# Two issuing queues at the start of a gated decode kernel, and the order of the first turnings

## The chip, the core and the metric

The kernel runs on one core of one Trainium2 chip. The metric is the device time of one execution in microseconds (us), the median of several runs. The engines are PE (matrix products; PEld is its weight load), DVE (vector), ACT (scalar functions), POOL and SP. SP and ACT can issue DMAs, each on a queue of its own; sixteen DMA engines move the data.

## The reference

One token goes through two branches, attention over a sliding window of a cache and a dense layer with gelu, mixed by a gate. Cut to what matters:

```python
# x: 1 x 576; 32 query heads, 16 key/value heads of 128; window W = 4096
q = (x @ wq)                                   # 576 x 4096 -> 32 heads
k = k_cache[:, :, Sk - W:, :]                  # 16 heads x 4096 x 128
v = v_cache[:, :, Sk - W:, :]
scores = einsum("bhqd,bhkd->bhqk", q, k) * Dh ** -0.5
a = (softmax(scores) @ v).reshape(1, 1, 4096) @ wo
b = gelu(x @ w1 + b1) @ w2 + b2                # 576 -> 4608 -> 576
g = sigmoid((x * gate_w).sum())
out = g * a + (1 - g) * b
```

All arrays are bf16. The window of keys and of values is 16.8 MB each, and with the weights 53.6 MB are read from HBM.

## The kernel before

**Tiles of keys and values.** The 16 key/value heads are taken four at a time: four tiles of keys (k0 to k3) and four of values (v0 to v3), 4 MB each. Every tile is one DMA (`load_kv`, L104): 128 partitions, each with one row of 32 KB. They take turns in a pool of three buffers (`kv_pool`, L80), which also holds the two halves of w2 at the end. So a tile can only be issued when an earlier one has been used up. The weights w_q, w1 and w_o share one buffer (`w_pool`, L81) in turn.

**Order of the DMAs.** All are issued by SP, in this order, except b2, which ACT issues (L140): the first part of w_q (512 KB), k0, x, the larger part of w_q (4096 KB), k1, b1 in two pieces, a row of x, gate_w, k2, then v0, k3, w1, v1, v2, v3, w_o and w2. The larger part of w_q comes behind k0 and x by `load_flat` (L120), which calls `first_keys` (L142) between its two pieces.

**x and the query.** x is loaded as 64 short rows of nine numbers, `x9` (L144). One product with `dup` (L384) and four DVE steps (L392) spread it over the partitions as `x2`, the stationary operand of the query products and later of w1. The query takes 36 products (L401), in nine steps over four column groups; the first four need only the first part of w_q, the other 32 the larger part. Then DVE and ACT copy the query from PSUM (L413, L419), 16 small products turn it (L425), and four DVE copies (L437) lay it into `qz`, the stationary operand of the scores.

**Turnings and scores.** A tile of keys is cut into four chunks (UT = 4). `transposes(h)` (L249) turns chunk h on DVE into a buffer `kT`, of which there are four (L83). `scores(h)` (L271) multiplies the chunk by `qz` in eight products. Chunks 0 to 3 are of k0, 4 to 7 of k1, and so on.

**What sets the order.** The schedule is by hand (`manual_schedule`, L90): every engine runs its instructions in the order of the program text. On DVE this is: constants, `transposes(0)`, the spread of x, `transposes(1)` to `transposes(3)`, the copies of the query, and then, chunk by chunk, the turning of the tile after the one whose scores are running, with the steps of the softmax (L290 to L322) between. `v0` is issued after `transposes(3)`, because it takes the buffer of k0; k3 after `transposes(7)`, v1 after `transposes(11)`, v2 after the products with v0 (`values(0)`), v3 after `transposes(15)`.

**The end.** After the values (L341) and their sums, `part` collects in PSUM (L672) half of w_o, the first half of w2 and the rest of w_o; DVE and ACT copy it (L680, L681). The second half of w2 comes in four pieces; its rows are multiplied one by one (L652), the copies of `part` are added by eight products after the thirteenth row (L692), and the result is copied (L701) and stored (L702).

Of the kernel before, what the change touches and what calls it, by code (L numbers as in the profile page):

```python
# [9 lines left out]
BF16 = mybir.dt.bfloat16  # L10
# [6 lines left out]
def kernel(  # L17
# [15 lines left out]
    nc = tc.nc  # L33

    P = 128
# [10 lines left out]
    UT = 4  # L46
# [9 lines left out]
    NQ = 4  # L56
# [6 lines left out]
    NM = 9  # L63


    QC = Hq * Dh // 8
# [14 lines left out]
    w_pool = ctx.enter_context(tc.tile_pool(name="w_pool", bufs=1))  # L81
# [11 lines left out]
    wq_flat = A_wq.rearrange("a b -> (a b)").rearrange("(p n) -> p n", p=P)  # L93
# [7 lines left out]
    def load_kv(cache, m, name):  # L101
        t = kv_pool.tile([P, NCK, Dh], BF16, name=name, tag="kv")

        nc.sync.dma_start(  # L104
            out=t[:],
            in_=cache[0, HT * m : HT * (m + 1), Sk - W : Sk, :].rearrange(
                "e (p c) d -> p e (c d)", c=NCK
            ),
        )
        return t  # L110

    def load_k(m):
        return load_kv(A_k_cache, m, "k_t")

    def load_v(m):
        return load_kv(A_v_cache, m, "v_t")

    WMAX = F * D // P

    def load_flat(src, name, cuts=(), between=None):  # L120
        n = src.shape[1]
        t = w_pool.tile([P, WMAX], BF16, name=name, tag="w")
        edges = (0, *cuts, n)
        for i, (a, b) in enumerate(zip(edges, edges[1:])):
            if i == 1 and between is not None:
                between()
            nc.sync.dma_start(out=t[:, a:b], in_=src[:, a:b])
        return t

    k_tiles, v_tiles = {}, {}  # L130

    x9 = const.tile([P // 2, NM], BF16, name="x9")
# [6 lines left out]

    nc.scalar.dma_start(out=b2_r[:], in_=B_b2.rearrange("(o n) -> o n", o=1))  # L140

    def first_keys():  # L142
        k_tiles[0] = load_k(0)
        nc.sync.dma_start(out=x9[:], in_=A_x.rearrange("a b (i m) -> (a b i) m", m=NM))  # L144

    wq_t = load_flat(wq_flat, "wq_t", (NQ * QC,), first_keys)

    k_tiles[1] = load_k(1)  # L150
    b1_r = const.tile([P, 2, FB], BF16, name="b1_r")
    nc.gpsimd.memset(b1_r[:], 0.0)
    for o in range(2):
        nc.sync.dma_start(
            out=b1_r[o : o + 32 * (NQ - 1) + 1 : 32],
            in_=B_b1.rearrange("(o t k n) -> o t k n", o=2, t=NQ, k=2)[o],
# [18 lines left out]
        out=row_f[:], in_=ident_f[:, 0 : 32 * (NQ - 1) + 1 : 32], axis=AX.X, op=ALU.add  # L175
# [5 lines left out]
        out=dup[:].rearrange("k (i e) -> k i e", e=2),  # L181
        in_=ident[0 : P // 2, 0 : P // 2].rearrange("k (i e) -> k i e", e=1).to_broadcast(
            [P // 2, P // 2, 2]
        ),
    )
    par = const.tile([P, 2], FP32, name="par")
    for o in range(2):
        nc.vector.tensor_reduce(
            out=par[:, o : o + 1],
            in_=ident_f[:].rearrange("p (i o) -> p o i", o=2)[:, o, :],  # L190
# [7 lines left out]
    for o in range(NOG):  # L198
        nc.vector.tensor_copy(
            out=spread_o[:, o, :].rearrange("k (t r q) -> k t r q", t=NT // NOG, q=QD),  # L200
            in_=ident[:, (P // NOG) * o : (P // NOG) * (o + 1)].rearrange("k (t x u) -> k t x u", x=32, u=1)[
                :, :, 0:R, :
            ].to_broadcast([P, NT // NOG, R, QD]),
# [5 lines left out]
        out=m_r[:, 0:R], in_=ident_f[:].rearrange("p (s r) -> p r s", r=R), axis=AX.X, op=ALU.add  # L209
# [8 lines left out]
        out=off[:], in_=ident_f[:].rearrange("p (x g q) -> p g x q", g=HT, q=2), axis=AX.XY,  # L218
# [3 lines left out]
        out=off[:], in0=off[:], scalar1=1.0e30, scalar2=-1.0e30, op0=ALU.mult, op1=ALU.add  # L222
# [4 lines left out]
        out=m_c[:], in_=ident_f[:].rearrange("p (t c r) -> p c t r", c=BC, r=R), axis=AX.XY,  # L227
# [4 lines left out]
        out=m_q[:], in_=ident_f[:].rearrange("p (h q) -> p q h", q=QD), axis=AX.X, op=ALU.add  # L232
# [7 lines left out]
        out=sel[:].rearrange("p l (o h) -> p l o h", o=2),  # L240
        in_=ident[:].rearrange("p (h l x) -> p l x h", h=2, l=2)[:, :, 0:2, :],
# [4 lines left out]
    def transposes(h):  # L246
        kT[h] = kT_pool.tile([P, NCH * ND], FP32, name="kT", tag="kT")
        lo = (h % UT) * NCH * Dh
        nc.vector.transpose(  # L249
            out=kT[h][:],  # L250
            in_=k_tiles[h // UT][:].rearrange("p c d -> p (c d)")[:, lo : lo + NCH * Dh].bitcast(
                FP32
            ),
        )
# [123 lines left out]

    transposes(0)

    x_ps = ps_m.tile([P, NM], FP32, name="x_ps", tag="m")
    nc.tensor.matmul(x_ps[:], lhsT=dup[:], rhs=x9[:], start=True, stop=True)  # L384
    ev, od = par[:, 0:1], par[:, 1:2]
# [5 lines left out]
    ):  # L391
        nc.vector.tensor_scalar(out=dst, in0=src, scalar1=s, scalar2=None, op0=ALU.mult)  # L392

    for h in range(1, UT):
        transposes(h)
    v_tiles[0] = load_v(0)

    q_ps = ps_a.tile([P, 2, 512], FP32, name="q_ps", tag="a")
    for b in range(NM * NQ):
        m, t = b // NQ, b % NQ  # L400
# [10 lines left out]
    for i in range(NI):  # L411
        copy = nc.scalar.copy if i % 2 else nc.vector.tensor_copy
        copy(  # L413
            out=q_r[:, i].rearrange("p (b o) a u -> p b o a u", b=2)[:, :, :, 0, :],
            in_=q_ps[:, 0, i * Dh : (i + 1) * Dh].rearrange("p (b u o) -> p b o u", b=2, o=2),
        )
    for i in range(NI):
        copy = nc.scalar.copy if i % 2 else nc.vector.tensor_copy
        copy(  # L419
            out=q_r[:, i, :, 1:NA, :],  # L420
            in_=q_r[:, i, :, 0:1, :].to_broadcast([P, NBP, NA - 1, PI]),
# [12 lines left out]
    for a in range(NA):  # L434
# [3 lines left out]
            out=qz[rows, lo : lo + NR * QW].rearrange("p (b t w) -> p b t w", b=NBP, w=QW)[  # L438
                :, :, :, 0:R
            ].rearrange("p b t (l i) -> p b t l i", l=2),  # L440
            in_=qT[rows].rearrange("p i b (l t) -> p b t l i", l=2),
# [115 lines left out]

    for h in range(UT):
        scores(h)
# [66 lines left out]
    for o in range(NOG):  # L629
# [3 lines left out]
        out=ow_m[:],  # L633
# [5 lines left out]
    with nc.allow_low_precision("one of the eight summands is not zero"):  # L639
        nc.vector.tensor_reduce(  # L640
            out=ow[:].rearrange("p j o -> p o j"),
            in_=ow_m[:].rearrange("p o q j -> p o j q"), axis=AX.X, op=ALU.add,
# [90 lines left out]
```

## Time and profile before

| | |
|---|---|
| median of 3 runs | 133.25 us (133.07 to 133.31) |
| the profiled execution | 133.64 us |
| its span, first to last instruction | 131.8 us |
| DVE busy | 73.9 us, 56% of the span |
| PE busy | 71.9 us, 55% |
| ACT busy | 9.6 us, 7% |
| read from HBM | 53.62 MB, 407 GB/s over the span |
| chain that ended last, by engine | DVE 35%, DMA 30%, PE 27% |

A group of the profile has a line (L401 is line 401 of the kernel), an engine, an operation and its operands. A timeline line gives start, duration, engine, line and operands, and in brackets how long the engine had stood idle before and what ended that. A line of waits gives who waited for whom: the sum in us, how many times, the longest. The chain of work that ended last is followed back from the last instruction to whatever released each step; it says what the end waited for, not what was busiest. The row of the DMA engines gives their busy share in tenths in 40 equal slices of the span.

### The profile page before, as it was taken

What the parts mean: (1) busy time and instruction counts of PE and PEld (TensorE: products, weight loads), DVE (VectorE), ACT (ScalarE), POOL (GpSimd) and SP (SyncE); (2) the same over time, 40 slices, a digit from 0 to 9 for tenths busy, and PEclk for the clock granted to TensorE, in tenths of its full rate; (3) what the DMA queues carried; (4) which work ended last, traced back from release to release, by engine and by line L of the source; (5) the groups of instructions that cost most, each with busy time, mean ns of one, the idle gap of its engine ahead of it and who ended that gap; (6) DMA issues with size and microseconds to landing.
All of it is one profiled execution on the core that took longest, in us unless ns stands there. A gap on an engine that the chain in (4) does not pass through costs nothing.

```text
span 131.8 us, 1417 instructions
## 1 busy us (share of the span) xinstructions
PE 71.9 (55%) x590; PEld 30.4 (23%) x590; DVE 73.9 (56%) x114; ACT 9.6 (7%) x19; POOL 3.9 (3%) x10
## 2 busy tenths in 40 slices
PE   0000010565999668805972882838936547646871
PEld 0000000222344224302431220213613122213441
DVE  2900599323199999995049907164758852670011
ACT  3200000012000002100300000030030000000011
POOL 8300000000000000000000000000000000000000
PEclk9999999999999999996897555555698555995599
DMA  4999998998999899999999999999999999999950
GB/s 103 514 408 408 458 418 388 478 458 369 450 468 433 378 468 448 408 410 512 403 428 403 453 408 438 468 413 408 458 448 398 463 403 475 385 416 420 419 224 0
DMA packets 2557, 53.70 MB, mean 408 GB/s; under 512 B 364, under 2 KB 632, under 8 KB 888
## 3 DMA queue, kind: packets, MB, share of 16 engines
q1 hardware_dynamic: 2550, 53.62, 95.2%
q8 instruction: 4, 0.07, 0.2%
q14 instruction: 1, 0.01, 0.0%
q10 hardware_dynamic: 2, 0.00, 0.0%
HBM read 53.62 MB, written 0.00 MB: 407 GB/s over the span
## 4 chain that ended last, share of the span: by engine, by line
DVE 35%; DMA 30%; PE 27%; issue 3%; SPq 1%; ACT 1%; DVEq 0%
DVE kT L249 20%; DMA wq_t<-in_A_wq_dram 17%; PE s_ps L271 15%; DMA w_t<-in_B_w_dram 13%; PE acc L341 4%; PE q_ps L401 3%; DVE ms L290 3%; PE h_ps L454 2%; DVE mx L295 2%; DVE ez L322 2%; DVE a_s L363 2%; DVE hT L479 1%; PE mb L312 1%; DVE qz L437 1%; PE mT L301 1%
## 5 line engine op out<-in xcount | busy, mean ns | idle before, releaser
L271 PE MATMUL s_ps<-kT,qz 128*128 128x512 bf16 x128 | 39.7, 473 | 10.7 <-DVE kT L249 9.4
L249 DVE STREAM_TRANSPOSE kT<-k_t 128x2048 f32<-128x2048 f32 x16 | 36.2, 2289 | 11.5 <-DMA k_t<-in_A_k_cache_dram 7.8
L271 PEld LDWEIGHTS <-qz 128*128 128x128 bf16 x128 | 14.2, 113 | 32.5 <-issue 22.5
L341 PE MATMUL acc<-v_t,ez 128*32 128x512 bf16 x128 | 11.2, 487 | 0.0
L401 PE MATMUL q_ps<-wq_t,x 128*32 128x512 bf16 x36 | 4.2, 626 | 9.0 <-DMA wq_t<-in_A_wq_dram 6.6
L316 ACT ACTIVATE pr<-ms,nb 128x1024 bf16<-128x1024 f32 x4 | 4.6, 1149 | 60.8 <-DVE nb L313 60.8
L384 PE MATMUL x_ps<-x,dup 64*128 64x9 bf16 x1 | 0.2, 163 | 14.8 <-DMA x<-in_A_x_dram 14.8
L371 PE MATMUL o_ps<-a_s,m_r 128*32 128x128 f32 x8 | 1.9, 319 | 8.2 <-DVE a_s L363 8.2
L290 DVE TENSOR_TENSOR ms<-s_ps,off 128x1024 f32<-128x1024 f32 x4 | 4.8, 1210 | 2.6 <-PE s_ps L271 2.5
L401 PEld LDWEIGHTS <-x 128*32 128x32 bf16 x36 | 1.4, 134 | 20.9 <-issue 20.9
L322 DVE STREAM_TRANSPOSE ez<-pr 128x1024 bf16<-128x1024 bf16 x4 | 4.9, 1220 | 1.4 <-ACT pr L316 1.4
L301 PE MATMUL mT<-ident_f,mx 128*1 128x128 f32 x4 | 1.3, 332 | 7.5 <-DVE mx L295 7.5
L341 PEld LDWEIGHTS <-ez 128*32 128x32 bf16 x128 | 4.2, 114 | 4.2 <-issue 2.5
L295 DVE TENSOR_REDUCE mx<-ms 128x1 f32<-128x1024 f32 x4 | 4.9, 1220 | 0.1
L313 DVE TENSOR_SCALAR nb<-mb 128x1 f32<-128x1 f32 x4 | 0.6, 145 | 7.7 <-PE mb L312 7.7
L680 DVE COPY part<-part 128x288 f32<-128x288 f32 x1 | 0.5, 458 | 7.6 <-PE part L672 7.6
L363 DVE SCALAR_TENSOR_TENSOR a_s<-acc,m_c,a_s 128x128 f32<-128x128 f32 x12 | 4.2, 351 | 0.4
L302 DVE TENSOR_REDUCE m<-mT 1x8 f32<-1x128 f32 x4 | 1.1, 268 | 5.2 <-PE mT L301 5.2
L672 PE MATMUL part<-wo_t,ow 128*1 128x288 bf16 x64 | 4.0, 395 | 0.0
L166 DVE CAST ident_f<-ident 128x128 f32<-128x128 bf16 x1 | 2.2, 2174 | 2.4 <-POOL ident masks.py:199 2.4
L359 DVE TENSOR_SCALAR a_s<-acc,m_c 128x128 f32<-128x128 f32 x4 | 1.3, 330 | 3.7 <-PE acc L341 3.7
L672 PE MATMUL part<-w_t,gt 128*1 128x288 bf16 x36 | 2.6, 440 | 1.5 <-DMA w_t<-in_B_w_dram 1.5
(85 smaller groups left out, 47.2 us busy)
## 6 DMA issues: line engine op xcount, KB each, us to landing
k_t<-in_A_k_cache_dram SPq DMA_DIRECT2D x4, 4096.0 KB, 24.8
v_t<-in_A_v_cache_dram SPq DMA_DIRECT2D x4, 4096.0 KB, 30.2
w_t<-in_B_w_dram SPq DMA_DIRECT2D x1, 5184.0 KB, 31.1
wo_t<-in_A_wo_dram SPq DMA_DIRECT2D x1, 4608.0 KB
wq_t<-in_A_wq_dram SPq DMA_DIRECT2D x1, 4096.0 KB, 22.1
w_t<-in_B_w_dram SPq DMA_DIRECT2D x1, 2592.0 KB, 18.4
w_t<-in_B_w_dram SPq DMA_DIRECT2D x1, 1872.0 KB, 15.5
w_t<-in_B_w_dram SPq DMA_DIRECT2D x1, 576.0 KB, 16.9
```

What stands on the lines that cost most here:

```text
L249: nc.vector.transpose(out=kT[h][:], in_=k_tiles[h // UT][:].rearrange("p c d -> p (c d)")[:, lo : lo + NCH * Dh].bitcast(FP32),)
L271: nc.tensor.matmul(s_tiles[t][:, k].rearrange("p c i e -> p c (i e)"), lhsT=qz[:, r * QW + lo : r * QW + lo + P], rhs=kT_v[:, k * NCB : (k ...
L290: nc.vector.tensor_tensor(out=ms[:], in0=s_v, in1=off[:].rearrange("p (o e) -> p o e", o=1).to_broadcast([P, NCH * 8, HT]), op=ALU.add,)
L295: nc.vector.tensor_reduce(out=mx[:], in_=ms[:].rearrange("p x e -> p (x e)"), axis=AX.X, op=ALU.max)
L301: nc.tensor.transpose(out=mT[:], in_=mx[:], identity=ident_f[:])
L316: nc.scalar.activation(out=pr[:].rearrange("p c j -> p (c j)"), in_=ms[:].rearrange("p x e -> p (x e)"), func=ACT.Exp, bias=nb[:, 0:1], sc ...
L322: nc.vector.transpose(out=ez[:, t].rearrange("p x c r -> p c x r"), in_=pr[:].rearrange("p c j -> p (c j)"),)
L341: nc.tensor.matmul(acc[t][32 * ct : 32 * ct + BC * R, :, :], lhsT=ez[:, t, x, c : c + BC, :].rearrange("p c r -> p (c r)"), rhs=v_tiles[t] ...
L363: nc.vector.scalar_tensor_tensor(out=a_s[:], in0=acc[t][:, c, :], scalar=m_c[:, c : c + 1], in1=a_s[:], op0=ALU.mult, op1=ALU.add,)
L401: nc.tensor.matmul(q_ps[32 * t : 32 * (t + 1), 0, 0:QC], lhsT=x2[:, m, :], rhs=wq_t[:, b * QC : (b + 1) * QC], start=(m == 0), stop=(m == ...
L454: nc.tensor.matmul(h_box[0][32 * t : 32 * (t + 1), k, 0:FB], lhsT=x2[:, m, :], rhs=w[:, off : off + FB], start=(m == 0), stop=(m == NM - 1),)
L672: nc.tensor.matmul(part[32 * t : 32 * t + 1, k, 0:DB], lhsT=col, rhs=w[:, i * D + k * DB : i * D + (k + 1) * DB], start=(n == 0 and t > 0) ...
```

## The change

ACT issues x and the larger part of w_q, on its own queue; SP issues the first part of w_q, k0 and k1 without them in between. In the program text the spread of x now stands ahead of all turnings, then come `transposes(0)` and `transposes(1)`, then the query, and `transposes(2)`, `transposes(3)` and the issue of v0 stand behind the query, right ahead of the first scores. Nothing is added or left out.

```diff
-    def first_keys():
-        k_tiles[0] = load_k(0)
-        nc.sync.dma_start(out=x9[:], in_=A_x.rearrange("a b (i m) -> (a b i) m", m=NM))
-    wq_t = load_flat(wq_flat, "wq_t", (NQ * QC,), first_keys)
+    wq_t = w_pool.tile([P, WMAX], BF16, name="wq_t", tag="w")
+    nc.sync.dma_start(out=wq_t[:, 0 : NQ * QC], in_=wq_flat[:, 0 : NQ * QC])
+    k_tiles[0] = load_k(0)
+    nc.scalar.dma_start(out=x9[:], in_=A_x.rearrange("a b (i m) -> (a b i) m", m=NM))
+    nc.scalar.dma_start(
+        out=wq_t[:, NQ * QC : wq_flat.shape[1]], in_=wq_flat[:, NQ * QC :]
+    )
     k_tiles[1] = load_k(1)
...
-    transposes(0)
-
     x_ps = ps_m.tile([P, NM], FP32, name="x_ps", tag="m")
     nc.tensor.matmul(x_ps[:], lhsT=dup[:], rhs=x9[:], start=True, stop=True)
...
-    for h in range(1, UT):
+    for h in range(2):
         transposes(h)
-    v_tiles[0] = load_v(0)
...
+    for h in range(2, UT):
+        transposes(h)
+    v_tiles[0] = load_v(0)
 
     for h in range(UT):
         scores(h)
```

## The prediction

> **What bounds the kernel now.** I read the DMA line of the page first, then the chain of work that ended last in order of time, then the waits of the last stretch.
>
> ```profile
> DMA  4999998998999899999999999999999999999950
> q1 hardware_dynamic: 2550, 53.62, 95.2%
> ```
>
> The 16 DMA engines are busy from the first slice to the last but two. The trace also keeps one record per DMA packet: one row of a 4 MB load is 32 KB and takes 1.21 us on its engine, the next row begins where the last ended, and I find no idle time from 2.7 us to 126 us. Whatever the kernel does, 53.6 MB need this long; nothing ends before the last piece of w2, which is used at 128.54.
>
> ```profile
> 2.50 22.13 DMA wq_t<-in_A_wq_dram
> ...
> 24.67 3.63 PE q_ps L401 x25
> ...
> 32.03 3.61 PE s_ps L271 x8
> ...
> 35.66 8.94 DVE kT L249 x4
> ...
> 107.80 3.44 PE acc L341 x27
> ...
> 111.64 16.86 DMA w_t<-in_B_w_dram
> ```
>
> This is the chain (start, duration, what). It begins with the landing of w_q at 24.62 and then holds no DMA at all until 111: query, scores, turnings, softmax and values follow each other with gaps of hundredths. So there are two bounds side by side: the full DMA queue, and a chain of arithmetic that starts when w_q is there. How far apart they are is read at the end, where the chain meets the last weights.
>
> ```profile
> PE part L672 <- DMA w_t<-in_B_w_dram: 1.5, 1, 1.5
> PE y_ps L652 <- DMA w_t<-in_B_w_dram: 1.1, 2, 0.7
> ```
>
> PE waits for w2 three times, 1.48 + 0.72 + 0.33 = **2.5 us**. That is the slack of the chain: what delays it by up to 2.5 us is hidden, each microsecond beyond is paid. The copies of `part` end at 127.07 and their product starts at 127.62, behind the thirteen rows on PE, so they don't shorten this slack.
>
> **The change, part by part.**
>
> *Issues.* SP loses x and the larger part of w_q (0.59 us each in its row) and issues the second keys at about 1.87 instead of 3.12; b1, x_row and gate_w move up as much, and gate_w still waits for the small loads. The third keys are issued when the first have landed (an SP wait of about 9 us that ended at 14.64 with that landing); SP stands still meanwhile. ACT issues b2 at 1.33 as before, then x at about 1.87 and w_q at about 2.5. Behind them on ACT stand only the table load (1.28 us) and the copy of b2 (needed near 117), so ACT's 1.2 us cost nothing. First packet: 1.03 us after the issue in w_q's first part. No byte is added, and the engines start at the same moment, so the DMA bound stays where it is: 0.
>
> *x.* It no longer queues behind 4 MB of keys. The spread (one product, 0.16, four DVE steps, 0.63) stood between the turnings at 14.84 to 17.50, hidden by the wait for w_q. It will stand ahead of them, hidden by the wait for keys: 0. The four early q products (0.62) likewise.
>
> *w_q.* Here lies the cost. Before, one queue served everything in order: first part, keys 0, x, w_q, keys 1. Now w_q has a queue of its own, and SP's queue goes on to **keys 1** as soon as keys 0 are through. On a full DMA each row of keys 1 that slips ahead of the last row of w_q delays the query by 1.21 us. So the question is how an engine divides itself between two queues. The nearest rows are the instruction fetches, which have queues of their own (q8 and q14):
>
> ```profile
> q8 instruction: 4, 0.07, 0.2%
> ```
>
> In the packet records the first of the four starts at 41.69 on an engine that has just moved 7 of the 8 rows of the third keys, and the eighth follows; the others start after 2 rows of a value load and after 6 rows of w_o; a q14 fetch at 57.27 after 4 rows of keys. So an engine changes queues between single rows, in the middle of a load. I take this as turns, one packet each, while both queues hold work. The order on one engine is then: keys row, x packet, keys row, x packet and so on; x has 64 packets of 18 bytes, 4 per engine, and one that signals, so it uses five turns, against five rows of keys 0. Then w_q's 8 rows and its signal alternate with what is left: 3 rows and the signal of keys 0, then 5 rows of keys 1 before w_q's signal. w_q lands at 24.62 + 5 x 1.21 = **30.7**. Lower end: x's packets pass together and w_q starts with the second row of keys; then at most one or two rows are ahead, 24.6 to 27. Upper end: w_q behind all of keys 1, at their landing, 34.3 (SP's wait from 24.80 for their buffer, 9.5). I take 30.7, the case that the fetch rows show. On the way keys 0 land at about 14.6 + 3 x 1.2 = 18.2, and their two turnings (4.5) are done at 22.8, before w_q: hidden.
>
> *Turnings 2 and 3 behind the query.* Before, the four turnings of keys 0 ended at 24.19, in the shadow of w_q. Now two of them stand after DVE's last copy of the query, 7.36 us after w_q's landing (24.62 to 31.98). DVE waited there 3.7 us for the first scores to give back a kT buffer:
>
> ```profile
> 35.66 8.94 DVE L249 STREAM_TRANSPOSE kT<-k_t 128x2048 f32<-128x2048 f32 x4 [3.69 <-PE s_ps L271]
> ```
>
> The two turnings take 2 x 2.24 = 4.5, the wait covered 3.7, so keys 1 are turned **0.8 us** later. The scores of chunk 2 need their turning 2.3 us after the query, and PE reaches them only after 5.5: no wait. From 44.6 on DVE has no idle time to give this back.
>
> *Sum.* The chain is late by (30.7 − 24.6) + 0.8 = 6.9 us; of this 2.5 are hidden at the end: **+4.3 us**, after rounding. The profiled execution took 133.64 for its span of 131.8; it becomes 138.0. It lies 0.4 above the median of 133.25, so I forecast **137.6**.
>
> *The queue under a late chain.* Loads that wait for buffers are issued later by the same 6.9. The tightest are the last values, issued at 89.26 when the last turning freed their buffer:
>
> ```profile
> 89.26 0.54 SPq L104 DMA_DIRECT2D v_t<-in_A_v_cache_dram  x1
> ```
>
> In the packet records the loads ahead of them end between 93.5 and 95.3, depending on the engine. Issued at 96.2, with 1.0 to 2.0 us to the first packets, they leave the slowest engine (the one that ends last at 128.4) idle for 2 to 3 us. The DMA bound thus moves by about 2.5, less than the 4.3 of the chain: it decides nothing, and the three waits in the tail go away.
>
> **A rule against the row.** The Trainium skill, "DMA: Bandwidth & Descriptors", section "Queues, rings and completion order", says that an engine goes round between queue rows and drains a whole packet, typically 9 to 17 descriptors, before it switches. A load's share here is nine (8 rows and a signal), so by that rule w_q would come after all of keys 1 and the sum would be the rival "late" below; the fetches after 7, 2, 6 and 4 rows speak against it, though they are of other queues.
>
> **The rivals.**
>
> *Fair share (ends on the other side), 20%.* x's tiny packets don't cost five turns, or w_q's descriptors come early enough to start beside the first rows of keys. For: b2, the only load on ACT's queue now, had its data and its signal served one right after the other at 3.94 and 3.99. Against: the keys may just not have been ready on that engine. Then w_q lands at 24.6 to 26, the chain is late by 0.8 to 2.2, and the 2.5 us hide it: 133.3, no change. It decides as long as w_q lands before 24.6 + 2.5 − 0.8 = 26.3.
>
> *In between, 8%.* One to three turns lost, w_q at 27 to 28.5: chain 3.2 to 4.7 late, 134 to 135.5.
>
> *Late, 9%.* The queues change only between whole loads, or descriptors are made in order of issue, so that keys 1 (SP, 1.87) are ahead of w_q (ACT, 2.5) and the second queue doesn't do what it is there for. w_q at 34.3: chain 10.5 late, 133.25 + 10.5 − 2.5 = 141.2.
>
> *Changing queues costs time, 7%.* After each of the five fetches the next row of q1 took about 0.5 us more (1.68 to 1.74 against 1.21 for 32 KB). If every row of the mixed stretch paid this, 16 rows x 0.47 = 7.5 us would be lost on the DMA bound itself and more on w_q: 141 to 145. Against: the key row behind b2's packets took its plain 1.21.
>
> *Faster, 4%.* Nothing in the sum takes time off the full DMA queue; even a w_q that lands much earlier would only lengthen PE's waits for w2. It would need a DMA that moves rows faster from two queues than 1.21 us, and between rows there is no gap to win.
>
> **How the numbers follow.** Forecast, turns with five lost, 52%: 137.6, by itself 136.4 to 139.0 (one turn more or less is 1.2 us, and PE's granted clock changes between 0.5 and 1.0 along the chain). Fair share 20%, of which 17 end within 0.2%; in between 8; late 9; switching 7; faster 4. Range 133.0 to 139.2: forecast, fair share and in between, 80%. By over 0.2% (0.27 us, about what a measurement of this kernel can tell from no change): faster 4%, within 18%, slower 78%.
>
> **What the new profile shows.** Right: w_q lands near 30.7 (end of the idle time of the q products), x near 10 to 11, keys 0 near 18; the scores start at about 38; keys 3 are issued near 51.5; the PE waits for w2 in the tail are gone. If w_q lands before 26 the time is unchanged and my turns are wrong. If it lands near 34 the switching is by loads. If single rows last longer than 1.21 us between 4 and 30 us, switching costs. Wrong in the sum: the tail still waits for w2 though w_q came late, or the turnings of keys 1 start without the 0.8.

## The result and the profile after

The changed kernel takes **138.25 us** (median of 4 runs, 137.22 to 140.20) against 133.27 before (4 runs): ratio 1.035, 95% interval 1.026 to 1.044. Executions that the chip disturbed (here the one at 140.20) are left out of every ratio in this document, and of the pairs of means in the experiments. The three that are left here took 137.22, 137.53 and 138.97, 4.7 us more than before in the mean. The profile is of the longest of them: 138.97 for a span of 137.2, 5.3 us above the profiled execution of before.

First the DMA lines of the page after, to set beside those of before.

```profile
DMA  4999899999893899799999899999999898999920
q1 hardware_dynamic: 2326, 49.43, 84.8%
q10 hardware_dynamic: 226, 4.20, 7.1%
```

ACT's queue (q10) now carries 4.2 MB. The row of the engines has a hole that was not there before: the 3 in the thirteenth slice, near 43 us. The second view is the chain of work that ended last (start, duration, what).

```profile
2.46 29.66 DMA wq_t<-in_A_wq_dram
...
32.16 3.63 PE q_ps L397 x32
...
39.50 5.76 DVE kT L248 x3
...
119.08 3.33 PE acc L340 x20
...
126.56 5.96 PE part L672 x90
```

w_q lands 29.7 us after its issue at 2.46, where it took 22.1 before. From there the chain runs to the end, and no further DMA stands in it: the piece `DMA w_t` that closed the chain before is gone. The waits of the last stretch say the same: PE waits for w2 nowhere, where it had waited three times. The timeline of the start, with the idle time ahead of an instruction and its releaser in brackets:

```profile
12.83 0.60 SPq L104 DMA_DIRECT2D k_t<-in_A_k_cache_dram  x1
12.86 0.16 PE L381 MATMUL x_ps<-x,dup 64*128 64x9 bf16 x1 [12.86 <-DMA x<-in_A_x_dram]
16.59 4.50 DVE L248 STREAM_TRANSPOSE kT<-k_t 128x2048 f32<-128x2048 f32 x2 [2.82 <-DMA k_t<-in_A_k_cache_dram]
32.16 3.61 PE L397 MATMUL q_ps<-wq_t,x 128*32 128x512 bf16 x32 [17.89 <-DMA wq_t<-in_A_wq_dram]
39.52 12.61 PE L270 MATMUL s_ps<-kT,qz 128*128 128x512 bf16 x48 [1.35 <-DVE qz L433]
44.03 0.58 SPq L104 DMA_DIRECT2D v_t<-in_A_v_cache_dram  x1
52.80 0.54 SPq L104 DMA_DIRECT2D k_t<-in_A_k_cache_dram  x1
```

x came 2 us earlier than before and keys 0 2 us later; w_q came 7.5 us later, and the scores with it. How far the chain is late, step by step:

| step | before | after | late by |
|---|---|---|---|
| query products start (w_q landed) | 24.67 | 32.16 | 7.5 |
| scores start | 32.03 | 39.52 | 7.5 |
| k3 issued (k1 turned) | 44.63 | 52.80 | 8.2 |
| v2 issued (products with v0 done) | 66.38 | 75.62 | 9.2 |
| v3 issued (k3 turned) | 89.26 | 95.58 | 6.3 |
| w_o issued | 96.06 | 101.15 | 5.1 |
| `part` starts (L672) | 118.77 | 126.49 | 7.7 |
| result copied by DVE (L701) | 129.13 | 134.54 | 5.4 |

By 53 us the chain is 8.2 us late, which is where it also stands at `part`, within half a microsecond. What is added and taken away in between goes with the clock that PE is granted, in the two stretches compared here. The stretch from v2's issue to v3's, before (after the stretch: its length, then busy time of PE, PEld, DVE, ACT, POOL, then PEclk, the granted clock, and the DMA share and GB/s):

```profile
66.30:89.26 22.96, 13.62 (x41) 4.96 (x38) 13.36 (x14) 1.41 (x3) 0.00 (x0) 0.59 1.01 437
103.94:118.77 14.83, 7.93 (x76) 2.95 (x77) 8.01 (x25) 0.23 (x1) 0.00 (x0) 0.73 0.98 419
```

and after, the same two pieces of work (v2 to v3, first issue of w2 to `part`):

```profile
75.50:95.60 20.10, 10.38 (x41) 4.33 (x38) 12.79 (x14) 1.41 (x3) 0.00 (x0) 0.81 0.99 424
110.07:126.56 16.49, 10.10 (x79) 3.56 (x83) 7.81 (x24) 0.00 (x0) 0.00 (x0) 0.60 0.98 418
```

In the first, PE had a clock of 0.81 in place of 0.59; its busy time was 3.2 us shorter and the stretch 2.9. In the second it had 0.60 in place of 0.73; its busy time was 2.2 us longer and the stretch 1.7.

**How an engine divides itself.** From 12.5 to 30 us, after:

```profile
q10 hardware_dynamic: 121, 3.96, 52.4%
q1 hardware_dynamic: 121, 3.44, 45.5%
```

121 packets each (those of q1 include the signals of keys 0, one per engine): the queues take turns. The trace's record of single packets shows it row by row. On nine engines the first packet of x goes at about 5.9, behind the second row of keys 0, on seven behind the third, at about 7.2; then one packet of x, one row of keys, and so on for 1.21 us each time. x's signal goes at 10.8 to 11.4 on the nine and 12.1 to 12.5 on the seven. w_q's first row follows at 12.0 to 12.6 on the nine, at 13.3 to 13.7 on the seven; its last row starts at 27.7 to 28.4 and at 29.0 to 29.4, its signal goes at 30.1 to 30.8 and at 31.5 to 31.8. Rows of this stretch last 1.213 us, as most rows did before.

**The hole.** v0 could only be issued at 44.03, because turnings 2 and 3, which free its buffer, now stand behind the query. The queue had run dry at 42.9.

```profile
42.00:44.00 2.00, 2.00 (x7) 0.75 (x6) 2.00 (x2) 0.00 (x0) 0.00 (x0) 1.00 0.00 0
44.00:46.00 2.00, 2.00 (x11) 0.89 (x10) 2.00 (x2) 0.00 (x0) 0.00 (x0) 1.00 0.60 164
```

The packet records have 3.1 us of idle time per engine here, and the first rows afterwards last up to 2.2 us in place of 1.21. (A packet is booked in the stretch in which it starts, so the shares are shifted a little.) The last row of w2 ended at 131.8, against 127.8 before: the DMA bound moved by 4.0 us.

### The profile page after: what moved, and what is told of

It reads as the page before. It is cut to its first block, busy times and chain, and to the rows that moved or that the text cites. A ratio compares the mean times of both kernels' runs of the same rounds, so it can differ in the third digit from the quotient of the medians.

```text
span 137.2 us, 1419 instructions
## 1 busy us (share of the span) xinstructions
PE 71.3 (52%) x590; PEld 30.9 (23%) x590; DVE 73.9 (54%) x114; ACT 9.6 (7%) x19; POOL 3.8 (3%) x10
## 4 chain that ended last, share of the span: by engine, by line
DVE 39%; PE 30%; DMA 22%; issue 5%; ACT 1%; POOL 0%; ACTq 0%; DVEq 0%; POOLq 0%
DMA wq_t<-in_A_wq_dram 22%; DVE kT L248 20%; PE s_ps L270 9%; PE acc L340 7%; PE part L672 4%; DVE ms L289 3%; DVE a_s L362 3%; DVE mx L294 3%; PE q_ps L397 3%; DVE ez L321 2%; PE y_ps L652 1%; PE part L665 1%; PE mb L311 1%; PE o_ps L370 1%; DVE hT L475 1%
## 5 line engine op out<-in xcount | busy, mean ns | idle before, releaser
L270 PE MATMUL s_ps<-kT,qz 128*128 128x512 bf16 x128 | 36.1, 441 | 11.1 <-DVE kT L248 9.7
L270 PEld LDWEIGHTS <-qz 128*128 128x128 bf16 x128 | 13.5, 108 | 30.3 <-issue 18.5
L340 PE MATMUL acc<-v_t,ez 128*32 128x512 bf16 x128 | 14.1, 591 | 0.0
L409 DVE CAST q_r<-q_ps 128x128 bf16<-128x128 f32 x2 | 0.6, 291 | 15.1 <-PE q_ps L397 14.7
L397 PEld LDWEIGHTS <-x 128*32 128x32 bf16 x36 | 1.5, 134 | 28.4 <-issue 28.3
L340 PEld LDWEIGHTS <-ez 128*32 128x32 bf16 x128 | 4.9, 135 | 6.0 <-issue 5.5
L672 PE MATMUL part<-wo_t,ow 128*1 128x288 bf16 x64 | 4.5, 436 | 0.0
L389 DVE TENSOR_SCALAR x<-x_ps,par 128x5 bf16<-128x5 f32 (+1 forms) x4 | 0.6, 231 | 6.3 <-PE x_ps L381 6.3
## 6 DMA issues: line engine op xcount, KB each, us to landing
wq_t<-in_A_wq_dram ACTq DMA_DIRECT2D x1, 4096.0 KB, 29.7
```

Of the source, the lines that this page charges most:

```text
L270: nc.tensor.matmul(s_tiles[t][:, k].rearrange("p c i e -> p c (i e)"), lhsT=qz[:, r * QW + lo : r * QW + lo + P], rhs=kT_v[:, k * NCB : (k ...
L340: nc.tensor.matmul(acc[t][32 * ct : 32 * ct + BC * R, :, :], lhsT=ez[:, t, x, c : c + BC, :].rearrange("p c r -> p (c r)"), rhs=v_tiles[t] ...
L397: nc.tensor.matmul(q_ps[32 * t : 32 * (t + 1), 0, 0:QC], lhsT=x2[:, m, :], rhs=wq_t[:, b * QC : (b + 1) * QC], start=(m == 0), stop=(m == ...
L672: nc.tensor.matmul(part[32 * t : 32 * t + 1, k, 0:DB], lhsT=col, rhs=w[:, i * D + k * DB : i * D + (k + 1) * DB], start=(n == 0 and t > 0) ...
```

## The experiments

Theories: the **chain theory** (w_q's late landing delays a chain of which 2.5 us are hidden) with the **turn theory** as its cause (one packet from each queue, and x's five packets cost five turns). Rivals: the **queue theory** (the hole near 44 is the cost), the **order theory** (the new order of the turnings is), the **share theory** (the queues share the bytes evenly, whatever the packets), and the **start theory** (ACT's queue starts late whatever stands in it). The experiments ran on other chips than the first result, where before varies more (133.0 to 137.0), so each ratio is against the kernel before on the same chip.

**Each half of the change alone.** Order only: the changed kernel with x and w_q back on SP.

```diff
-    nc.scalar.dma_start(out=x9[:], ...)
-    nc.scalar.dma_start(out=wq_t[:, NQ * QC : ...], ...)
+    nc.sync.dma_start(out=x9[:], ...)
+    nc.sync.dma_start(out=wq_t[:, NQ * QC : ...], ...)
```

> SP issues everything as before; only the order of DVE and of the first values' load is the new one. Chain theory (the time is set by the chain that starts at the landing of w_q, 2.5 us of it hidden at the end): w_q lands at 24.6, the two turnings behind the query make the chain 0.7 to 0.8 us late, which is hidden: 133.3 us, no change, and PE still waits for w2 at the end. Order theory (the new order by itself is what costs, since the first values are issued some 12 us later and the turnings stand on the path): 135 to 138 us.

Measured 133.85 us beside 134.14 before (means), ratio 0.998 (0.992 to 1.003). The tail still waits for w2:

```profile
PE part L672 <- DMA w_t<-in_B_w_dram: 3.3, 1, 3.3
PE y_ps L652 <- DMA w_t<-in_B_w_dram: 0.6, 1, 0.6
```

The order by itself costs nothing that can be measured; the order theory falls. ACT's issues only, as against the changed kernel:

```diff
+    transposes(0)
     x_ps = ps_m.tile([P, NM], FP32, name="x_ps", tag="m")
...
-    for h in range(2):
+    for h in range(1, UT):
         transposes(h)
+    v_tiles[0] = load_v(0)
...
-    for h in range(2, UT):
-        transposes(h)
-    v_tiles[0] = load_v(0)
```

> ACT issues x and w_q as in the changed kernel, but the turnings and the first values' load keep their old places, ahead of the query. Chain theory: w_q lands at 32.1 again, the first values are issued near 26 and the DMA engines have no gap near 44; the chain is late by 7.5 us, of which 2.5 are hidden: 137.5 to 138.5 us, as the changed kernel. Queue theory (the 3 us in which the DMA engines stood idle near 44 us, because the first values were issued at 44.0, are the cost): with that gap gone, 133.5 to 135.5 us.

Measured 138.96, ratio 1.032 (1.023 to 1.041): the whole loss. v0 is issued at 29.2 (26 was expected), and the engines are busy through 46:

```profile
42.00:44.00 2.00, 2.00 (x7) 0.61 (x5) 0.64 (x1) 0.00 (x0) 0.00 (x0) 1.00 0.91 393
44.00:46.00 2.00, 2.00 (x10) 0.87 (x9) 1.97 (x2) 0.00 (x0) 0.00 (x0) 1.00 0.91 393
...
96.00:98.00 2.00, 0.87 (x3) 0.31 (x3) 2.00 (x2) 0.20 (x2) 0.00 (x0) 0.50 0.00 0
```

The loss is there without the hole near 44, and the queue theory falls in this form. But the late chain made other holes, near 53 and here near 97, as k3 and v3 were issued late. In the packet records the engines stand idle 4.3 us in all here, against 3.1 in the changed kernel, the last row of w2 ends at 133.1, and PE still waits for it:

```profile
PE y_ps L652 <- DMA w_t<-in_B_w_dram: 1.3, 2, 0.8
```

So the two experiments show that ACT's issues cause the loss. They do not show by which way it is paid: a late chain costs directly and through loads that wait for buffers, and in this profile the loads ended last, in that of the changed kernel the chain.

**The turns.** x on SP ahead of the first keys, w_q alone on ACT:

```diff
+    nc.sync.dma_start(out=x9[:], ...)
     k_tiles[0] = load_k(0)
-    nc.scalar.dma_start(out=x9[:], ...)
```

> As the changed kernel, but x is issued by SP ahead of the first keys; ACT issues w_q alone. Turn theory (an engine gives each queue one packet at a time, so the five packets of x cost five rows of keys before w_q may start): w_q starts beside the first or second row of keys and lands at 25.0 to 27.0; chain late by 1.2 to 3.2, so 133.3 to 134.0 us. Start theory (ACT's loads come late for a reason of their own, such as descriptors made in order of issue): w_q still lands at 30 or later and the time stays above 136 us.

```profile
26.40 3.21 PE L397 MATMUL q_ps<-wq_t,x 128*32 128x512 bf16 x32 [16.50 <-DMA wq_t<-in_A_wq_dram]
...
PE part L672 <- DMA w_t<-in_B_w_dram: 2.5, 1, 2.5
...
PE y_ps L652 <- DMA w_t<-in_B_w_dram: 0.8, 2, 0.5
```

w_q landed at 26.40, as the turn theory has it. 135.77 us, ratio 1.008 (1.003 to 1.012): 0.4 to 1.6 us over before, where at most 0.7 was expected. The profile has the excess in the DMA, not the chain: PE waits 3.3 us for w2 at the end. Here w_q starts ahead of the keys, its first rows between 3.4 and 5.2 us and those of keys 0 between 5.9 and 8.9; rows up to 9 us last up to 2.4 us, and the engines stand idle for 0.6 us in this stretch. Why is not shown.

Then x behind the first keys, its old place, with w_q alone on ACT. The first four runs (133.32 to 136.04, w_q landing at 26.4 in the longest, which was profiled) gave no interval; the kernel was run again.

```diff
     k_tiles[0] = load_k(0)
-    nc.scalar.dma_start(out=x9[:], ...)
+    nc.sync.dma_start(out=x9[:], ...)
```

> As the changed kernel, but x goes on SP's queue right behind the first keys, its old place; ACT issues the larger part of w_q alone. Turn theory: without x's five packets ahead of it w_q starts beside the second or third row of keys and lands at 24.5 to 26, x with the keys near 22 to 25; chain late by 0.8 to 2.5 us, hidden: within 0.5 us of before. Start theory (a large load on ACT's queue is late by itself, whatever stands ahead of it): w_q at 30 or later and 137 us or more.

> x behind the first keys on SP's queue, w_q alone on ACT's, once more for an interval. Turn theory: w_q lands at 23.5 to 26, x with the first keys near 24 to 26.5, so the query starts 1 to 3 us later than before and the chain is 1.8 to 3.5 us late with the turnings behind it: hidden up to 2.5, so 0 to 1.0 us over before. Against it: if w_q alone on a second queue costs by itself, over 2 us.

134.01 beside 133.72 (means), ratio 1.003 (0.998 to 1.007). The DMA issues of the second profile (KB, us from issue to landing) and the timeline:

```profile
wq_t<-in_A_wq_dram ACTq DMA_DIRECT2D x1, 4096.0 KB, 23.2
...
x<-in_A_x_dram SPq DMA_DIRECT2D x1, 1.1 KB, 23.5
```

```profile
25.37 0.17 PE L381 MATMUL x_ps<-x,dup 64*128 64x9 bf16 x1 [25.37 <-DMA x<-in_A_x_dram]
```

Issued near 1.9, w_q landed near 25.1, x at 25.37; the scores start 2.2 us later than before, and this is hidden. One tiny load moved to the other queue takes back all of the loss that can be measured. The start theory falls as the cause of the loss.

Rows half as long: the first two tiles of keys in two DMAs each.

```diff
     def load_k(m):
+        if m > 1:
+            return load_kv(A_k_cache, m, "k_t")
+        t = kv_pool.tile([P, NCK, Dh], BF16, name="k_t", tag="kv")
+        for lo in range(0, NCK, NCK // 2):
+            nc.sync.dma_start(out=t[:, lo : lo + NCK // 2, :], in_=...)
+        return t
```

> As the changed kernel, but the first two tiles of keys are each loaded by two DMAs of half rows (16 KB in place of 32 KB a row). Turn theory: each turn of x and of w_q now costs half a row of keys; x lands near 9 to 10, w_q starts near 9 and takes 8 x (1.21 + 0.61) us: it lands at 23.5 to 25.0, the first keys near 24; 133.3 us, no change from before. Share theory (two queues with work share the bytes evenly, whatever the packets): w_q lands near 32 as in the changed kernel, 137 to 139 us.

```profile
10.45 0.17 PE L391 MATMUL x_ps<-x,dup 64*128 64x9 bf16 x1 [10.45 <-DMA x<-in_A_x_dram]
...
25.04 3.60 PE L407 MATMUL q_ps<-wq_t,x 128*32 128x512 bf16 x32 [13.17 <-DMA wq_t<-in_A_wq_dram]
```

x at 10.45, w_q at 25.04, each within half a microsecond of what was expected; 134.34 beside 134.14 (means), ratio 1.001 (0.995 to 1.006). With ACT's loads just as in the changed kernel, halving the *other* queue's rows brings w_q 7 us earlier. Shares by bytes would have left it at 32, so the share theory falls.

x behind w_q on ACT's queue:

```diff
-    nc.scalar.dma_start(out=x9[:], ...)
     nc.scalar.dma_start(out=wq_t[:, NQ * QC : ...], ...)
+    nc.scalar.dma_start(out=x9[:], ...)
```

> As the changed kernel, but ACT issues w_q first and x behind it. Turn theory: w_q starts beside the second or third row of keys and lands at 26 to 28, but the five packets of x now take their turns against rows of the second keys, and x lands five to six rows later, at 32 to 34; the spread of x (1 us) is then on the path, so the time is that of the changed kernel or 1 us more, 138 to 139.5 us. Start theory (ACT's large load is late for its own reason, x isn't): w_q at 31 or later, x near 32.

```profile
wq_t<-in_A_wq_dram ACTq DMA_DIRECT2D x1, 4096.0 KB, 23.9
...
x<-in_A_x_dram ACTq DMA_DIRECT2D x1, 1.1 KB, 29.5
```

w_q lands at 25.8, and x, 1.1 KB, at 31.9, about 6 us behind it: the same five turns, paid at the other end. 139.63 us, ratio 1.046 (1.037 to 1.056), just above the 138 to 139.5 that was expected.

**The slack.** Before, with n turnings of chunk 7 more than needed (n = 1 and 3):

```diff
     w1_t = load_flat(w1_flat, "w1_t")
+    for _ in range(n):
+        nc.vector.transpose(out=kT[2 * UT - 1][:], in_=k_tiles[1][...])
     chain = softmax(0)
```

> The kernel before, with chunk 7 of the keys turned once more than needed, on DVE between the issue of w1 and the first softmax: the chain is made 2.24 us longer at a place where DVE has no idle time, and no DMA is moved. Slack theory (2.5 us of the chain are hidden behind the waits for w2): no change within 0.3 us, and the PE waits for w2 at the end shrink to about 0.3 us. If the chain alone set the time: 135.5 us on a chip with 133.3 before.

> The same with three turnings more, 6.7 us: slack theory 6.7 - 2.5 = 4.2 us more than before (137.5 on a chip with 133.3), PE's waits for w2 gone; up to 2 us less if PE's clock is granted earlier along the later chain. If the end were set by the DMA queue alone: about 2 us more, from the last values' load that is issued 6.7 us later.

One more turning: 134.03 beside 134.02 (means), ratio 1.000 (0.995 to 1.005). In its profile, of an execution of 135.13, PE still waits 1.4 us for w2, where 0.3 was expected. Three: ratio 1.038 (1.030 to 1.045), 4 to 6 us more where 4.2 were expected. 2.2 us are hidden, 6.7 are not. How the second is paid is not clean: its profile has holes where k3 is late,

```profile
52.00:54.00 2.00, 0.00 (x0) 0.00 (x0) 1.97 (x2) 0.00 (x0) 0.00 (x0) 0.50 0.08 33
54.00:56.00 2.00, 0.00 (x0) 0.00 (x0) 1.97 (x2) 0.00 (x0) 0.00 (x0) 0.50 0.70 246
```

and a wait of 2.4 us for w2 at the end, where none was expected, so that in it the queue ended last (an execution of 140.27, above the median).

**The floor.** x and the whole of w_q on SP ahead of the keys:

```diff
-    wq_t = w_pool.tile(...)
-    nc.sync.dma_start(out=wq_t[:, 0 : NQ * QC], ...)
+    nc.sync.dma_start(out=x9[:], ...)
+    wq_t = load_flat(wq_flat, "wq_t", (NQ * QC,))
     k_tiles[0] = load_k(0)
-    nc.scalar.dma_start(out=x9[:], ...)
-    nc.scalar.dma_start(out=wq_t[:, NQ * QC : ...], ...)
```

> SP issues x, the whole of w_q, and only then the keys; the order of DVE is the new one. w_q lands near 14.5, 10 us earlier than before, the first keys near 24.6. Floor theory (nothing ends before the full DMA queue has moved 53.6 MB): no change, 133.0 to 133.6 on a chip with 133.3 before, though the chain runs about 4 us ahead; PE's waits for w2 at the end grow to 4 us or more. If the chain set the time: 129 to 131 us.

w_q landed at 15.0; 133.93, ratio 1.001 (0.998 to 1.005). The expected picture of the chain was wrong: the copies of the query stand on DVE behind two turnings that wait for keys until 24.7, so k3 was issued at 46.1, later than before, and PE's waits did not grow. So this run does not test the floor. The next has all four turnings behind the query as well:

```diff
-    for h in range(2):
-        transposes(h)
...
-    for h in range(2, UT):
+    for h in range(UT):
         transposes(h)
```

> As the kernel with x and the whole of w_q ahead of the keys on SP's queue, and all four first turnings behind the query, so that the query no longer waits on DVE behind turnings that wait for keys. w_q lands near 15, the query is laid out near 22, the first scores start near 27 (5 us earlier than before), and the third tile of keys' successor is issued some 2 us earlier than before. Floor theory: no change all the same, 133.0 to 133.6 us where before has 133.3, because the DMA queue is full; PE waits 2 us longer for w2 at the end. If the chain set the time: 131 to 132 us.

```profile
PE part L665 <- DMA w_t<-in_B_w_dram: 4.0, 1, 4.0
...
PE part L665 <- DMA wo_t<-in_A_wo_dram: 1.2, 1, 1.2
...
PE y_ps L645 <- DMA w_t<-in_B_w_dram: 0.2, 1, 0.2
```

Scores at 26.9, 5 us earlier than before, k3 issued at 43.2, 1.4 us earlier; 134.02 beside 134.24 (means), ratio 0.999 (0.994 to 1.003). What was won ends in waits of PE for w2 and w_o, 5.4 us in place of 2.5. Neither order beats the kernel before.

**The changed kernel again.**

> The changed kernel once more, beside the two others on one chip. Turn theory: x lands at 12.5 to 13.5 and w_q at 31.5 to 33 again, 137 to 140 us; no PE wait for w2 at the end, and the time goes with the clock that PE is granted along the chain, which it did not before.

138.87, ratio 1.033 (1.022 to 1.044). x at 13.1, w_q at 32.4, no wait for w2. Its four runs by mean granted clock: 0.863 138.38, 0.850 138.67, 0.838 139.08, 0.839 139.41. The three of the first result do not line up so well: 0.861 137.22, 0.851 138.97, 0.846 137.53. So that the time goes with the clock is not shown.

## Why the prediction was right, and where it was not

**What bounds it.** Right: a full queue and, beside it, a chain from w_q with some 2.5 us of slack. The one extra turning was hidden, and scores 5 us earlier won nothing. The size of the slack is that of one execution: in profiles of kernels whose time did not move PE waits 1.2 us (w_q ahead of the keys) to 3.9 us (order only) for w2.

**Issues and x: 0.** Right for ACT's time. The third keys waited for x's landing (12.83), not for the first keys'; nothing came of it. x was forecast for 10 to 11, late for the reason that follows.

**w_q at 30.7.** The mechanism was right, five turns for x and then row against row. The count was short: it let x's first packet go behind the first row of keys 0, and it went behind the second (nine engines) or the third (seven). On the seven, which set the landing at 32.1, 15 rows of keys go ahead of w_q's signal where the forecast had 13, and two rows are 2.4 us. That the term was off by only 1.4 (7.5 us in place of 6.1) is luck. It was counted from a landing of 24.62, and that was set by a single engine, whose first row of keys 0 took 2.12 us before: w_q's signal went at 24.3 there and between 23.2 and 23.8 on the other fifteen.

**Turnings, 0.8.** Measured 8.17 - 7.49 = 0.7.

**Sum.** 6.9 late less 2.5 was to give 4.3 or 4.4; `part` starts 7.7 late, less 2.5 is 5.2, and the profiled execution is 5.3 longer. That the rule fits to a tenth has luck in it: the lateness swung between 9.2 and 5.1 on the way, and the mean of the three runs is 4.7 above before, not 5.3.

**The queue.** Here a step was wrong: "The tightest are the last values". The change moves the issue of v0 behind turnings 2 and 3, and the forecast's account of the loads left it out. It went from 24.22 to 44.03, past the end of the queue at 42.9, and made the hole of 3.1 us; v3 found the queue almost full. The bound of the DMA moved by 4.0, not 2.5. "It decides nothing" held for this profile, by 1.4 us: the span grew by 5.4, of which the late loads alone would, by this estimate, have cost 4.0. It did not hold for the two kernels with holes elsewhere.

**Rivals.** Fair share: fell; its time and its landing of w_q are what the kernel with x behind the keys on SP's queue has. Changing queues: rows of the mixed stretch lasted 1.213 us, so the 0.5 us belongs to instruction fetches, not to changing. Late: fell, and with it, for these two queues, the rule of the Trainium skill ("DMA: Bandwidth & Descriptors", "Queues, rings and completion order") in the reading that the prediction gave it. Read as a whole share of nine before a switch it would have put w_q at 34; the trace has a switch after every row, 121 packets against 121.

**What stays open.** Why the first packets of x on ACT's queue start 4.0 us after their issue, where SP's first packets need 1.0. The packet records narrow it. In all seven profiles with keys 0 issued first, the load that ACT issues behind b2 starts at 4.9 to 5.9 us, whether it is x or w_q; in the one in which SP issues keys 0 only at 1.80, behind x, w_q starts at 3.4, 1.5 us after its issue. And with half rows four rows of keys go ahead of x on the first engines, not two, so it is a stretch of time or an amount of bytes, not a number of turns. This late start is the part of w_q's term that the forecast missed. Of the loss, how much comes through the chain and how much through late loads was not separated by an experiment: no spare buffer was there to issue the loads early.

## What to carry to other kernels

No run here gained from a second issuing queue on full DMA engines, and the queue took away the order. On each engine the two queues got one packet each in turn, whatever the size, so a load of tiny rows ahead of a large one cost a full row of the other queue for each of its packets on that engine and for its signal. If a load starts the longest chain, leave it in one queue ahead of what may come later, or at least put no tiny load ahead of it on its own queue. And when a step is moved, move the loads that wait for its buffers in the account too.

## What the runs showed of the hardware

- SP's and ACT's queues alternated by packets on each engine even when one held packets of 18 bytes and the other of 32 KB. Between large rows the change cost nothing (1.213 us a row, as alone), while after an instruction fetch the next row of 32 KB took 1.68 to 1.74 us.
- After the 3 us in which the engines were dry, the first rows lasted up to 2.2 us in place of 1.21. In the kernel with x ahead of the keys and w_q alone on ACT, rows that started between 3.4 and 9 us lasted up to 2.4 us.
- The same stretch of work (v2's issue to v3's) took 23.0 us at a granted clock of 0.59 before and 20.1 us at 0.81 after, so a lateness that is read in the middle of a kernel can hold microseconds that come from the clock.
